# Reordering the loads and the weight splitting at the start of a delta-rule attention and feed-forward kernel

## The chip, the cores and the metric

The kernel runs on one core of one Trainium2 chip. The metric is the device time of one execution in microseconds (us); lower is better. A core has a tensor engine (PE), VectorE (DVE), ScalarE (ACT), GpSimd (POOL) and SyncE (SP), each with an instruction stream of its own that runs strictly in order, and 16 DMA engines that serve the transfers which SP, ACT and POOL issue.

## What is computed

For each of 4 x 8 heads (768 tokens, 48 numbers each) a state matrix is carried along the tokens; the result is reshaped to 3072 tokens of 384 numbers and goes through a feed-forward part:

```python
k_n = k / (norm(k) + 1e-6)
for t in range(S):
    y[t] = q[t] @ state
    state = state + beta[t] * outer(k_n[t], v[t] - state.T @ k_n[t])
x = y, heads side by side                      # (3072, 384)
h = maximum(x @ w_in, 0)                       # w_in (384, 2048)
out = (h * h) @ w_out                          # w_out (2048, 384)
```

The two weight matrices arrive as 64-bit floats, the rest as 32-bit floats.

## The kernel before

**Units.** The tokens are cut into 12 units of 64. Within a unit the recurrence is written as a triangular system: products of keys with keys give a matrix whose 32 x 32 diagonal blocks are inverted, and the inverse (`T`, tile `tt`) is applied to the values. The steps of a unit `d` are: `load` (keys into `kpad`), `load_q`, `load_beta`, `load_v`; `normalize` (squares on ACT at line 268, a chain of small DVE operations, and the scaling of the keys at line 281); `static` (transposes at line 315, copies to `kq` at line 318, products at line 331, copies to `ap` at line 365 for the keys and 375 for the queries, GpSimd selections at line 378); `to_blocks` (line 349), which stores the key products to memory, and `from_blocks` (line 357), which loads their blocks as `lt`; `invert` (lines 417 to 429: a scaling, 31 pairs of DVE operations, a scaling; then the stores at line 433 and the loads at lines 444 and 449 that bring `tt` and `t1t`); `state_part` (`whole`, from the DVE transpose at line 460, `solved`, `onward`); and `moe`, the feed-forward part, from its transposes at line 568 on.

**The two first units.** Units 0 and 1 are inverted together: one `lt` tile holds unit 0's blocks in its lower 64 partitions and unit 1's in its upper 64, and one pass of `invert(ds_[0])` works on both. Their queries sit in `qpad` and in `kpad[2]`, so `load(2)`, which writes the keys of unit 2 to `kpad[2]`, comes after unit 1's queries were transposed.

**Weights.** The weights are 28 pieces in the order in which `moe` needs them: three of `w_in` (128 x 512 numbers, 512 KB) and four of `w_out` (128 x 384, 384 KB), four times over. `fetch(n)` issues the next n transfers on SP. `split_weights` is a generator that turns a piece into a high and a low part: `least` (ACT, line 136) scales the lower words, `words` (four DVE operations, lines 144 to 150) forms the parts, `high` (ACT, line 156), and `low` (tensor engine, lines 163 and 164, and an ACT copy, line 165) forms the low part. While `split_early` holds, one step of the generator takes one piece; afterwards a piece takes three steps, and a further DVE operation (line 170) replaces a matmul.

**Order.** The order of the work is written out by hand at the end of the function (lines 666 to 751), and each engine keeps it. `take(g, n)` runs n steps of a generator. Before, the first 6 weight pieces and unit 0's queries are issued among the key loads, 7 pieces are split before the inverse is written into the order, all 28 pieces are issued before the inverse's stores, 4 pieces are split between the inverse and `whole(ds_[0])`, and 6 within `state_part(ds_[0])` (`EARLY`). The remaining 11 are woven into the stage of unit 1 in `NS` steps, spread over the first 0.88 of the stage beside `moe(ds_[0])`. From then on the stage of unit u weaves `moe` of unit u-1, the state part of unit u, and the inverse of unit u+1.

Of the kernel before, what the change touches and what calls it, by code (L numbers as in the profile page):

```python
# [20 lines left out]
def kernel(  # L21
# [90 lines left out]
    halves = {}  # L112

    rooms = [(spool, "a", "rest"), (mpool, "r", "h_l")]
    AHEAD = 19

    def fetch(n):
        for _ in range(n):
            x = len(raws)
            if x < NW:  # L120
                src = weight_parts[x][2]
                raw = wpool.tile([P, src.shape[1], 2], I32, name=place[x])
                nc.sync.dma_start(out=raw.rearrange("p a b -> p (a b)"), in_=src.bitcast(I32))
                raws.append(raw)
# [5 lines left out]
    def split_weights():  # L130


        def least(x):

            w1 = raws[x][:, :, 1].bitcast(F32)
            nc.scalar.activation(out=w1, in_=w1, func=AF.Copy, scale=DOWN)  # L136
            return x,
# [34 lines left out]
        before, ready, x = None, [], 0  # L172
        while split_early:

            far = 3 if x < AHEAD - 3 else 1
            while len(ready) < far:
                ready.append(least(x + len(ready)))
            if x == 0:
                yield
            now = high(*words(*ready.pop(0)))  # L180
            if before:
                low(*before)
            before = now
            x += 1
            while len(ready) < (far if x < AHEAD - 3 else 1):
                ready.append(least(x + len(ready)))
            yield

# [2 lines left out]
        for x in range(x, NW):  # L191
            if before:
                remainder(*before)
            now = words(*ready.pop(0))
            yield
            if not ready and x + 1 < NW:
                ready.append(least(x + 1))
            yield
            if before:
                low(*before, formed=True)  # L200
            before = high(*now)
            yield
# [35 lines left out]
    def load_q(d):  # L238

        d["qp"] = kpad[2] if d["u"] == 1 else qp  # L240
        load_to(d["qp"], q, d, D)
# [390 lines left out]
    def take(gen, n=None):  # L632
        while n is None or n > 0:
            try:
                next(gen)
            except StopIteration:
                return
            if n is not None:
                n -= 1
# [23 lines left out]
        onward(d)  # L663
        yield

    F0, F1, F2 = 3, 3, 6
    EARLY = (2, 1, 2, 1)
    NS = 3 * (NW + 1 - (1 + 6 + 4 + sum(EARLY))) + 2
    STEPS = 32
    OVER = 4  # L670
    CHAIN = (14.9, 18.4, 21.9, 25.4)
# [6 lines left out]
    engines = {mybir.EngineType.PE, mybir.EngineType.SP, mybir.EngineType.DVE, mybir.EngineType.Activation}  # L678
    with tc.manual_schedule(engines=engines):
        ds_.append(load(0))  # L680
        fetch(F0 - 1)
        ds_.append(load(1))
        fetch(1)
        load_beta(ds_[0])
        load_q(ds_[0])
        load_beta(ds_[1])
        fetch(F1)
        take(normalize(ds_[0]))
        take(normalize(ds_[1]))
        take(splits, 1)  # L690
        pair = [static(d) for d in ds_[:2]]
        for d in pair:
            take(d, 2)
        for d in pair:
            take(d, 1)
        fetch(1)
        for d in pair:
            take(d, 1)
        fetch(2)
        load_q(ds_[1])  # L700
        fetch(F2 - 2)
        load_v(ds_[0])
        take(splits, 1)
        for d in pair:

            take(d, 2)
            take(splits, 1)
            take(d, 1)
            take(splits, 1)
            take(d, 1)  # L710
            take(splits, 1)
        ds_.append(load(2))
        fetch(NW)
        take(invert(ds_[0]))
        load_v(ds_[1])
        load_q(ds_[2])
        load_beta(ds_[2])
        third = normalize(ds_[2])
        take(third, 3)
        for _ in range(3):  # L720
# [61 lines left out]
```

## Time and profile before

| what | us |
|---|---|
| median of three runs | 657.76 |
| lowest and highest run | 652.09, 661.04 |
| profiled execution | 651.91 |
| its span, first to last instruction | 650.1 |

The profiled execution is one run; what it takes outside its span is 1.8 us. Positions in the text are microseconds from the start of this span. PE was busy for 91% of it, VectorE for 66% and ScalarE for 49%.

### The profile page before, as it was taken

How to read it: one execution, taken by the hardware profiler on the slowest of the kernel's cores; microseconds unless marked ns; L12 is line 12 of the kernel's file. 1: busy time of each engine (PE TensorE's matmuls, PEld its weight loads, DVE VectorE, ACT ScalarE, POOL GpSimd, SP SyncE). 2: the span in 40 equal slices, each digit the busy share in tenths (PEclk: the TensorE clock that was granted, in tenths of full speed). 3: DMA queues.
4: the chain of work that ended last, by engine and by line, in shares of the span. 5: the costliest groups of instructions: out<-in, count | busy, mean ns of one | idle time of the engine just before them, and what ended most of it. 6: DMA issues, size and time to landing. Idle time of an engine off the chain costs nothing.

```text
span 650.1 us, 22961 instructions
## 1 busy us (share of the span) xinstructions
PE 588.4 (91%) x9898; PEld 550.0 (85%) x9898; DVE 426.7 (66%) x1154; ACT 315.5 (49%) x620; POOL 37.3 (6%) x61
## 2 busy tenths in 40 slices
PE   0850689889999999999999999999999999999997
PEld 0530268778999999999999999999999999999997
DVE  3889778878479488487496594794884974842221
ACT  3731487555543553645454545435446454444442
POOL 6110000000100100101001001001000010000000
PEclk9956798889999999999999999999999999999999
DMA  7698632401541622722523525317226135030100
GB/s 159 155 247 307 199 63 53 66 3 26 98 70 27 121 58 35 117 52 46 100 52 59 90 45 103 65 28 123 55 41 113 28 51 92 3 63 5 25 2 25
DMA packets 173725, 49.92 MB, mean 77 GB/s; under 512 B 165424, under 2 KB 168504, under 8 KB 173624
## 3 DMA queue, kind: packets, MB, share of 16 engines
q1 hardware_dynamic: 171160, 47.85, 36.8%
q8 instruction: 78, 1.28, 0.8%
q10 hardware_dynamic: 2336, 0.59, 0.5%
q14 instruction: 23, 0.19, 0.1%
q0 software_dynamic: 128, 0.01, 0.0%
HBM read 37.32 MB, written 11.01 MB: 74 GB/s over the span
## 4 chain that ended last, share of the span: by engine, by line
PE 82%; DMA 8%; SPq 3%; DVE 3%; ACT 2%; issue 1%; ACTq 0%; DVEq 0%
PE o L589 32%; PE h L602 31%; DMA w<-in_moe_w_out_dram 2%; PE x L526 2%; PE g L502 2%; PE x L331 2%; PE x L502 2%; PE x L542 2%; DMA kpad<-in_k_dram 2%; PE g L331 2%; PE g L551 1%; SPq L230 1%; DMA inv<-tt 1%; PE x L477 1%; PE h L467 1%
## 5 line engine op out<-in xcount | busy, mean ns | idle before, releaser
L589 PE MATMUL o<-w,h_h 128*128 128x384 f32 x768 | 203.5, 346 | 0.0
L581 DVE TENSOR_TENSOR h_l<-r,h_h 128x512 fp32r<-128x512 f32 x96 | 66.5, 693 | 162.0 <-PE o L589 83.6
L602 PE MATMUL h<-x_h,w 128*128 128x256 f32 x1152 | 171.2, 285 | 0.0
L609 ACT ACTIVATE r<-h 128x512 f32<-128x512 f32 x96 | 57.5, 598 | 219.8 <-PE h L602 219.6
L602 PEld LDWEIGHTS h<-x_h,w 128*128 128x128 f32 x1152 | 156.7, 191 | 1.0
L589 PEld LDWEIGHTS o<-w,h_h 128*128 128x128 f32 x768 | 133.8, 188 | 3.2
L589 PE MATMUL o<-w,h_l 128*128 128x384 f32 x384 | 129.8, 338 | 0.0
L602 PE MATMUL h<-x_l,w 128*128 128x256 f32 x576 | 100.8, 284 | 0.0
L426 DVE SCALAR_TENSOR_TENSOR tmp<-lt,bt,z 128x126 f32<-128x126 f32 (+22 forms) x310 | 95.6, 308 | 7.3
L427 DVE TENSOR_TENSOR z<-z,tmp 128x126 f32<-128x126 f32 (+22 forms) x310 | 79.2, 255 | 10.7
L602 PEld LDWEIGHTS h<-x_l,w 128*128 128x128 f32 x576 | 83.0, 192 | 0.0
L589 PEld LDWEIGHTS o<-w,h_l 128*128 128x128 f32 x384 | 72.2, 188 | 0.0
L610 ACT ACTIVATE r<-r 128x512 f32<-128x512 f32 x96 | 60.7, 632 | 3.0
L612 ACT CAST h_h<-r 128x512 fp32r<-128x512 f32 x96 | 59.5, 620 | 3.1
L410 POOL MEMSET z<- 128x512 f32 x10 | 5.3, 532 | 441.2 <-DMA inv<-z 398.1
L163 PE MATMUL o<-r,plus 128*128 128x512 f32 (+1 forms) x16 | 10.5, 745 | 17.7 <-DVE r L146 17.7
L315 PE MATMUL x<-plus,kpad 64*128 64x64 f32 x104 | 7.5, 245 | 13.9 <-DVE kpad L281 13.9
L331 PE MATMUL x<-kq 48*64 48x64 f32 (+1 forms) x608 | 19.1, 248 | 0.2 <-ACT w L165 0.2
L163 PEld LDWEIGHTS o<-r,plus 128*128 128x128 f32 x16 | 3.0, 233 | 19.2 <-ACT s L271 16.0
L271 ACT ACTIVATE s<-n 128x16 f32<-128x16 f32 x12 | 2.6, 216 | 34.1 <-DVE n L269 34.1
L331 PEld LDWEIGHTS x<-kq 48*64 48x64 f32 x608 | 16.5, 145 | 2.9 <-issue 0.7
L136 ACT ACTIVATE w<-w 128x384 f32<-128x384 f32 (+1 forms) x28 | 17.0, 613 | 2.9 <-DMA w<-in_moe_w_out_dram 2.9
(131 smaller groups left out, 692.9 us busy)
## 6 DMA issues: line engine op xcount, KB each, us to landing
w<-in_moe_w_in_dram SPq DMA_DIRECT2D x12, 512.0 KB
w<-in_moe_w_out_dram SPq DMA_DIRECT2D x16, 384.0 KB
lt<-blocks SPq DMA_DIRECT2D x22, 256.0 KB
vt<-in_v_dram SPq DMA_DIRECT2D x48, 96.0 KB
out_dram<-a SPq DMA_DIRECT2D x46, 96.0 KB
kpad<-in_k_dram SPq DMA_DIRECT2D x88, 48.0 KB
qpad<-in_q_dram SPq DMA_DIRECT2D x88, 48.0 KB
blocks<-ap SPq DMA_DIRECT2D x48, 64.0 KB
```

Source lines behind the costliest of these rows:

```text
L136: nc.scalar.activation(out=w1, in_=w1, func=AF.Copy, scale=DOWN)
L163: nc.tensor.matmul(ps, lhsT=m, rhs=y, start=(m is first[0][0]), stop=False)
L331: nc.tensor.matmul(ps[j][to * C:(to + 1) * C, p, (x - first) * C:(x - first + m) * C], lhsT=kq[rows, c, p, b, 0], rhs=kq[rows, c, p, b, x: ...
L426: nc.vector.scalar_tensor_tensor(out=tmp, scalar=bt[:, s:s + 1], op0=ALU.mult, op1=ALU.mult, **factors)
L427: nc.vector.tensor_tensor(out=z[:, :nj, s + 1:], in0=z[:, :nj, s + 1:], in1=tmp, op=ALU.subtract)
L502: nc.tensor.matmul(dst[j][to, c, p], lhsT=d["kq"][rows, c, p, b, x], rhs=state[rows, b, c, p], start=(c == 0 and p == 0) if x else True, s ...
L581: nc.vector.tensor_tensor(out=h_l, in0=r, in1=h_h.bitcast(F32), op=ALU.subtract)
L589: nc.tensor.matmul(o[i], lhsT=a[:, e, i * P:(i + 1) * P], rhs=halves["wo", ft][w], start=(ft == 0 and n == 0), stop=(ft == FT - 1 and n == 2))
L602: nc.tensor.matmul(hp[:, e], lhsT=halves["wi", (kt, ft // EACH)][w][:, f], rhs=x[:, kt], start=(n == 0), stop=(n == 3 * KT - 1))
L609: nc.scalar.activation(out=r, in_=hp, func=AF.Relu)
L610: nc.scalar.activation(out=r, in_=r, func=AF.Square)
L612: nc.scalar.copy(out=h_h, in_=r)
```

## The change

Both units' keys are issued first; three weight pieces follow. ACT scales no longer three pieces ahead but two. `static` of unit 0 is run as far as `to_blocks` before unit 1's transposes. Four pieces (not seven) are split before the inverse, with one scaled in the first step. Both units' queries, unit 0's values and pieces up to the fifteenth are issued between `from_blocks` and the inverse, and the other 13 pieces behind the loads of `T`, among unit 2's queries, unit 1's values and unit 2's betas. `NS`, the number of weaving steps in the stage of unit 1, goes from 38 to 44, since 14 pieces are left for it where 11 were. `AHEAD` now only says from which piece on both scratch buffers are no longer used in turn.

```diff
-    AHEAD = 19
+    AHEAD = 17
...
         while split_early:
-            far = 3 if x < AHEAD - 3 else 1
-            while len(ready) < far:
-                ready.append(least(x + len(ready)))
             if x == 0:
+                ready.append(least(x))
                 yield
             now = high(*words(*ready.pop(0)))
...
-            while len(ready) < (far if x < AHEAD - 3 else 1):
+            while len(ready) < 2:
                 ready.append(least(x + len(ready)))
             yield
...
-            if not ready and x + 1 < NW:
-                ready.append(least(x + 1))
+            if x + 2 < NW:
+                ready.append(least(x + 2))
...
-    NS = 3 * (NW + 1 - (1 + 6 + 4 + sum(EARLY))) + 2
+    NS = 3 * (NW - (4 + 4 + sum(EARLY))) + 2
...
         ds_.append(load(0))
-        fetch(F0 - 1)
         ds_.append(load(1))
-        fetch(1)
         load_beta(ds_[0])
-        load_q(ds_[0])
+        fetch(3)
         load_beta(ds_[1])
-        fetch(F1)
         take(normalize(ds_[0]))
         take(normalize(ds_[1]))
+        pair = [static(d) for d in ds_[:2]]
+        take(pair[0], 2)
         take(splits, 1)
-        pair = [static(d) for d in ds_[:2]]
-        for d in pair:
-            take(d, 2)
-        for d in pair:
-            take(d, 1)
+        take(pair[0], 1)
+        take(pair[1], 2)
+        take(splits, 1)
         fetch(1)
+        take(pair[1], 1)
+        take(splits, 1)
         for d in pair:
             take(d, 1)
         fetch(2)
+        take(splits, 1)
+        load_q(ds_[0])
+        take(splits, 1)
+        fetch(3)
         load_q(ds_[1])
-        fetch(F2 - 2)
+        fetch(2)
         load_v(ds_[0])
-        take(splits, 1)
+        fetch(4)
         for d in pair:
-            take(d, 2)
-            take(splits, 1)
-            take(d, 1)
-            take(splits, 1)
-            take(d, 1)
-            take(splits, 1)
+            take(d)
         ds_.append(load(2))
+        take(invert(ds_[0]))
+        fetch(2)
+        load_q(ds_[2])
+        fetch(3)
+        load_v(ds_[1])
+        load_beta(ds_[2])
         fetch(NW)
-        take(invert(ds_[0]))
-        load_v(ds_[1])
-        load_q(ds_[2])
-        load_beta(ds_[2])
         third = normalize(ds_[2])
```

## Rows read from the trace of the kernel before

**Rows 1.** The page, parts 1 and 2: busy time of the tensor engine (share of the span, instructions), and its busy tenths in 40 slices of 16.25 us each.

```profile
PE 588.4 (91%) x9898; PEld 550.0 (85%) x9898; DVE 426.7 (66%) x1154; ACT 315.5 (49%) x620; POOL 37.3 (6%) x61
...
PE   0850689889999999999999999999999999999997
```

**Rows 2.** Busy time of each engine in three stretches, cut where the tensor engine begins the transposes of a unit for the feed-forward part (line 568: unit 0 at 93.0 us, unit 1 at 157.0, unit 2 at 202.4). Columns: stretch and its length, then busy us and instructions of PE, PE weight loads, VectorE, ScalarE, GpSimd, then granted clock, DMA share, GB/s.

```profile
0.00:93.00 93.00, 46.17 (x704) 29.21 (x705) 69.87 (x162) 42.01 (x95) 17.16 (x34) 0.80 0.74 196
93.00:157.00 64.00, 53.58 (x831) 48.45 (x830) 51.70 (x126) 38.30 (x77) 0.00 (x0) 0.92 0.24 39
157.00:202.40 45.40, 45.40 (x829) 43.77 (x828) 31.68 (x93) 22.25 (x43) 2.36 (x3) 1.00 0.40 70
```

**Rows 3.** The chain that ended last, in order of time: start, length, what held it.

```profile
1.66 2.98 DMA kpad<-in_k_dram
...
27.62 3.30 DMA blocks<-ap
30.98 0.51 SPq L357
...
63.93 8.22 DMA inv<-tt
```

**Rows 4.** ScalarE's timeline: start, length, line, operation, output and input; in brackets the idle time before and what ended it.

```profile
9.46 0.94 ACT L268 ACTIVATE rest<-kpad 128x384 f32<-128x384 f32 x2 [5.97 <-DMA kpad<-in_k_dram]
...
13.00 0.94 ACT L268 ACTIVATE rest<-kpad 128x384 f32<-128x384 f32 x2 [1.73 <-DMA kpad<-in_k_dram]
...
14.87 1.73 ACT L136 ACTIVATE w<-w 128x512 f32<-128x512 f32 x3
16.50 0.56 ACT L318 COPY kq<-x 128x512 f32<-128x512 f32 x1
...
18.68 0.58 ACT L318 COPY kq<-h 128x512 f32<-128x512 f32 x1 [1.13 <-PE x L315]
...
19.77 0.37 ACT L365 COPY ap<-x 128x256 f32<-128x256 f32 x1
...
22.77 0.38 ACT L365 COPY ap<-x 128x256 f32<-128x256 f32 x1
```

**Rows 5.** VectorE's timeline, in the same columns.

```profile
12.83 0.96 DVE L281 TENSOR_TENSOR kpad<-kpad,s 128x768 f32<-128x768 f32 x1 [0.15 <-DMA kpad<-in_k_dram]
...
16.50 0.96 DVE L281 TENSOR_TENSOR kpad<-kpad,s 128x768 f32<-128x768 f32 x1
17.37 0.42 DVE L144 TENSOR_SCALAR a<-w 128x512 int32<-128x512 int32 x1
...
19.62 0.42 DVE L144 TENSOR_SCALAR r<-w 128x512 int32<-128x512 int32 x1
...
35.84 1.23 DVE L417 TENSOR_TENSOR lt<-lt,bt 128x1024 f32<-128x1024 f32 x1
...
46.09 0.74 DVE L427 TENSOR_TENSOR tt<-tt,h_h 128x247 f32<-128x247 f32 x1
...
47.66 0.42 DVE L427 TENSOR_TENSOR tt<-tt,h_h 128x252 f32<-128x252 f32 x1
...
48.57 0.88 DVE L427 TENSOR_TENSOR tt<-tt,h_h 128x255 f32<-128x255 f32 x1
...
61.97 1.23 DVE L429 TENSOR_TENSOR tt<-tt,bt 128x1024 f32<-128x1024 f32 x1
...
74.74 0.56 DVE L150 SCALAR_TENSOR_TENSOR rest<-w 128x384 fp32r<-128x384 uint32 x1
78.62 0.45 DVE L460 STREAM_TRANSPOSE t<-t1t 128x256 f32<-128x256 f32 x1 [3.32 <-DMA t1t<-inv]
...
108.94 0.35 DVE L144 TENSOR_SCALAR a<-w 128x384 int32<-128x384 int32 x1
...
119.44 0.42 DVE L144 TENSOR_SCALAR a<-w 128x512 int32<-128x512 int32 x1
```

**Rows 6.** SyncE's timeline of transfers issued: start, length over all, line, output and input, count.

```profile
0.81 2.76 SPq L230 DMA_DIRECT2D kpad<-in_k_dram  x4
...
32.63 6.23 SPq L230 DMA_DIRECT2D kpad<-in_q_dram  x8
...
44.02 6.96 SPq L230 DMA_DIRECT2D kpad<-in_k_dram  x8
...
63.93 1.71 SPq L433 DMA_DIRECT2D inv<-tt  x2
72.22 1.93 SPq L444 DMA_DIRECT2D tt<-inv  x4
...
81.15 2.73 SPq L224 DMA_DIRECT2D vt<-in_v_dram  x4
```

**Rows 7.** GpSimd's timeline: the selections that mask the second unit's query products.

```profile
45.66 1.69 POOL L378 TENSOR_SCALAR_AFFINE_SELECT ap<-ap 64x512 f32<-64x512 f32 x2 [13.70 <-ACT ap L375]
48.53 1.44 POOL L378 TENSOR_SCALAR_AFFINE_SELECT ap<-ap 64x512 f32<-64x512 f32 x2 [1.18 <-ACT ap L375]
```

**Rows 8.** Busy time in the stretch 60 to 70 us, columns as in group 2.

```profile
60.00:70.00 10.00, 4.67 (x7) 1.79 (x8) 9.24 (x26) 2.57 (x6) 0.00 (x0) 0.50 1.03 411
```

**Rows 9.** Groups of instructions of the stretch 93 to 157 us by line: busy us, mean ns of one, then the idle time of the engine just before them and what ended it.

```profile
L163 PE MATMUL x<-w,plus 128*128 128x384 f32 (+1 forms) x11 | 5.1, 463 | 8.4 <-DVE w L170 6.1 <-DVE vt L510 2.2
...
L164 PE MATMUL x<-rest,plus 128*128 128x384 f32 (+1 forms) x11 | 4.2, 383 | 0.0
```

More of the change, by code (lines that the diff above doesn't have):

```diff
@@ L664, in state_part @@
         yield
-    F0, F1, F2 = 3, 3, 6
     EARLY = (2, 1, 2, 1)
-    NS = 3 * (NW + 1 - (1 + 6 + 4 + sum(EARLY))) + 2
+    NS = 3 * (NW - (4 + 4 + sum(EARLY))) + 2
     STEPS = 32
```

## The prediction

> **What bounds the kernel now.** I read the page first: the tensor engine is busy for 91% of the span, and its row of slices is at nine tenths from about 150 us to the end; only the first nine slices are thin [rows 1]. The change touches nothing after the stage of unit 1, so the question is when that later part can start. A table by stage says how much there is to win [rows 2]: from 157.0 us a stage lasts 45.4 us and PE is busy for all of it. Before that lie 93.0 us in which PE works 46.17, and a stage of unit 1 of 64.0 us, 18.6 longer than a later one, with VectorE busy for 51.70.
>
> Next the chain that ended last [rows 3] and the timelines of VectorE and SyncE [rows 5, 6]. In the first 93 us the path runs: keys, normalization, key products, their way through memory into `lt`, the inverse on VectorE (35.84 to 63.20, that is 27.36), the inverse's stores, the loads of `tt` and `t1t`, the DVE transpose of line 460 at 78.62, and the state part up to 93.0. Two stalls stand out. From 63.93 the stores of the inverse hold the chain for 8.22; in 60 to 70 us the DMA engines are full (share 1.03, 411 GB/s [rows 8]) with weight pieces issued ahead of those stores. And VectorE stands 3.32 before line 460, for `t1t` [rows 5].
>
> **The change part by part.** I follow four points: start of the inverse, its end, line 460, and the start of unit 0's feed-forward (93.0).
>
> *Start of the inverse (35.84 now).* SP issues a key transfer every 0.69 (2.76 for four [rows 6]), and one lands about 3 after its issue began (2.98 [rows 3]). With nothing but keys in front, two queues of eight are issued by 0.81 + 8 x 0.69 = 6.3, say 6.5 on ACT, whose squares of unit 0 stand behind its issues: 6.6 instead of 9.46 [rows 4]. Squares to scaling of unit 0 take 12.83 - 9.46 = 3.4, and unit 1's scaling follows 3.67 later [rows 5]: 10.0 and 13.7, ended 14.6, if unit 1's keys are there by 10 (they may come up to 2 later, behind the three pieces; before, its squares waited until 13.00 [rows 4]). ACT's first copies of transposed keys (16.50) wait now for three scalings of weights, 14.87 to 16.60 [rows 4]; these go behind them, and the copies come at about 12.6, bound by the transposes: unit 1's scaling ends at 16.50 + 0.96 = 17.46, its copies start at 18.68, 1.2 later [rows 4, 5]. Two copies (1.1), products, and four copies of products (half of 19.77 to 23.15, so 1.7 [rows 4]) put unit 0's stores at about 17. But one inverse serves both units, so what counts is unit 1: two copies, one cast and two scalings (some 0.6 each [rows 4]) and four copies more, about 4.5, so its stores start near 21.5, are issued by 23.7, land 3.3 after the last began (27.62 + 3.30 [rows 3]), at 26.9 or so, and its `lt` load is issued by 27.5. Its landing: from 30.98 to 35.84 is 4.9 at most [rows 3, 5], a key's 2.98 at least. I take 3.5, for only one weight piece stands near it: **31.0**, with ends 29 and 34. VectorE is not late: four pieces (three of 17.37 to 19.62 = 2.25, one narrow of about 1.9 by the ratio of 0.35 to 0.42 of their first operations [rows 5]) from 14.6 with waits for their scalings end near 27. The three pieces it no longer splits here return below.
>
> *Its end (63.20 now).* Length 27.36, but GpSimd stretches it. The operation of line 427 at 46.09 takes 0.74 where a larger one at 47.66 takes 0.42, and at 48.57 one takes 0.88 [rows 5], each beside a GpSimd selection [rows 7]. Now unit 0's four selections run before the inverse and unit 1's four within; after the change all eight queries' selections fall within, since `load_q` of both stands behind `lt`. Four more at about 0.35: +1.4 (bounds 0 and 3.1, the whole of four selections at 0.78). End 31.0 + 27.4 + 1.4 = **59.8**, 3.4 earlier.
>
> The Trainium skill (SBUF — State Buffer, section on the two separate sides) says that the port pair that VectorE and GpSimd share is an exclusive lock, and that the loser blocks for the whole instruction. The rows show operations stretched by 0.3 to 0.5, less than a selection's 0.78. By the rule taken literally the sum would be 1.7 higher than mine.
>
> Is SP free by then? From 27.8 it issues 2 + 3 + 2 + 4 pieces at some 0.5, two sets of queries (6.23), values (2.7) and unit 2's keys (6.96) [rows 6]: 27.6 in all, so 55.4. That is covered by 4.4; each us beyond would delay the stores by one.
>
> *Line 460 (15.4 behind the end now).* Two things must be ready. The transfers: the stores are no longer behind weights. The first load of `tt` starts at 72.22, 8.3 after the stores' issue at 63.93; on idle DMA engines I price that like the stores of blocks, 3.30, and 0.5 for the second store, and 72.22 to 78.62 = 6.4 stays: 0.2 + 3.8 + 6.4 = 10.4. VectorE: it now fills the wait with unit 2's normalization and four pieces until 75.30 [rows 5], 12.1 behind the end. After the change these are pieces 4 to 7, one wide and three narrow instead of three wide and one narrow: 12.1 - 2 x 0.3 = 11.5. So what is late next is VectorE, and line 460 comes at 59.8 + 11.5 = **71.3**: of the 5 us that the transfers save, 3.9 are had.
>
> *Start of unit 0's feed-forward (93.0).* 78.62 to 93.0 is 14.4 with six pieces in it; these have one wide piece fewer: 14.1. **85.4**, so 7.6 earlier.
>
> *The stage of unit 1.* It gets 14 pieces instead of 11. The 18.6 by which it exceeds a later stage, over 11 pieces, is 1.7 each [rows 2]: 3 x 1.7 = **+5.1**. From below: PE's own share, (5.1 + 4.2)/11 = 0.85 each [rows 9], 2.5. From above: between 108.94 and 119.44 VectorE begins a piece every 3.5 [rows 5], 10.5 for three. I take the middle, since VectorE is busy for 81% of the stage: neither free nor full. PE waits for the pieces here (8.4 ahead of line 163, 6.1 of it for VectorE [rows 9]).
>
> *The 13 late pieces.* Cost nothing, if covered: `T`'s loads occupy SP for 81.15 - 72.22 = 8.9 [rows 6], so from about 63.7 to 72.6; with queries, values, betas and pieces SP has issued the last at about 92, and eight pieces of 3.5 MB need 8.6 at 411 GB/s [rows 8]. Piece 20, first of these, lands near 94 and is scaled a quarter into the stage, near 102. If SP slips by more than 8, ACT waits there, and all its copies with it.
>
> Sum: -7.6 + 5.1 = **-2.5** on the profiled execution's 651.91, that is 649.4. That execution was near the fastest of the runs; against their median of 657.76 the same step gives **655.3**.
>
> **The rivals.** *Pieces nearly free.* VectorE has 12.3 idle in the stage [rows 2]; if the moved pieces fall there, only PE's 2.5 remains: -5.1, 652.7 (with an inverse at 29, -7.1). For: in this stage VectorE's idle time is in waits that more pieces can fill. Against: its first part has none.
>
> *VectorE bounds the stage of unit 1* (the other side). Place: the weave of pieces, inverse and remainders behind 85 us. If the stage is VectorE's, each piece costs its spacing, 3.5, and 10.5 - 7.6 = +2.9: 660.7. It decides once a piece costs over 2.5. For: 81% busy, PE waiting for it. Against: later in the stage it waits for PE.
>
> *The first blocks' early departure does nothing.* Both halves of `lt` are scaled at once, and unit 1's way is now behind unit 0's products. If its `lt` lands at 35.8 as before, the inverse ends at 64.6 and line 460 at 76.1, 2.5 earlier; with 0.3 and +5.1: +2.3, 660.1. For: the shared tile. Against: the keys and ACT's scalings ahead of it move by 3 to 4.
>
> **How the numbers follow.** Forecast 0.47, pieces nearly free 0.27, VectorE's stage 0.18, blocks late 0.08. By these the step lies between -8 and +3, 649.8 to 660.8; the three runs shown spread from 5.7 below to 3.3 above their median, so some of that goes on both ends: 646 to 662. The forecast's own range is -5 to 0. Two per cent, about what a measurement of this kernel can tell from no change, is 13 us: faster by that would need the whole gain, a free stage and a lucky set of runs, 0.07; slower by that needs the full price of the pieces and late weights, 0.04; the rest, 0.89, lies within.
>
> **What would show it.** Right: line 417 at 29 to 33; the inverse some 28.8 long with eight selections beside it; stores to first `tt` load in under 4.5; line 460 at 70 to 73 with no wait for `t1t` ahead of it; line 568 first at 84 to 87; then 67 to 71 us to unit 1's line 568. Wrong: line 417 still near 35; SP reaching the stores late; or ACT waiting for weight pieces of `w_out` behind 95 us. A stage of unit 1 of 66 us or less means the first rival, of 74 the second.

## The result: 0.56% slower, and where the time went

| what | before | after |
|---|---|---|
| median of 20 runs, us | 653.89 | 657.44 |
| lowest and highest run, us | 650.76, 661.04 | 654.70, 661.73 |
| profiled execution, us | 651.91 | 661.73 |
| start of unit 1's feed-forward in it (line 568 before, 566 after), us | 157.0 | 161.0 |

The ratio is 1.0056 with a 95% interval of 1.0036 to 1.0076: a small loss, where a small gain was forecast. The 657.76 us from which the prediction started was the median of three runs; twenty give 653.89. So 655.3 lies near 657.44 by luck, because the base was high, and the step, -2.5 for a measured +3.55, has the wrong sign.

In the code after, all lines from 230 on have numbers lower by two: 417 is 415, 460 is 458, 568 is 566. The page first, as in [rows 1]: PE is busy for 593.5 us where it was 588.4, and its thin slices now reach to the tenth.

```profile
PE 593.5 (90%) x9892; PEld 555.4 (84%) x9892; DVE 430.8 (65%) x1157; ACT 316.4 (48%) x620; POOL 36.1 (5%) x61
...
PE   2553878778999999999999999999999999999997
```

The stretches of after, cut at the same points as [rows 2] (line 566: unit 0 at 84.4 us, unit 1 at 161.0, unit 2 at 206.5), and one later stage. Columns as there.

```profile
0.00:84.40 84.40, 43.35 (x694) 27.71 (x694) 64.27 (x150) 38.19 (x86) 16.88 (x34) 0.78 0.70 170
84.40:161.00 76.60, 59.04 (x839) 53.45 (x838) 60.82 (x143) 42.96 (x86) 0.00 (x0) 0.87 0.37 83
161.00:206.50 45.50, 45.50 (x831) 43.88 (x830) 31.14 (x90) 22.32 (x43) 2.30 (x3) 1.00 0.41 69
298.80:347.60 48.80, 47.32 (x829) 45.43 (x828) 31.96 (x93) 22.25 (x43) 1.96 (x3) 0.97 0.37 65
```

The first stretch is 8.6 shorter, the second **12.6 longer**: 4.0 lost at 161.0, which the medians confirm with 3.55. The other 5.8 by which the two profiled executions differ are in later stages, where both kernels do the same. After's profiled execution is the slowest of its 20, with a stage of 48.8 in it, and the medians do not bear this part out; the last section returns to it.

The steps of the first stretch, in VectorE's timeline (start, length, line, operation, idle time before), to be held against [rows 5]:

```profile
30.29 1.23 DVE L415 TENSOR_TENSOR lt<-lt,bt 128x1024 f32<-128x1024 f32 x1 [3.37 <-DMA lt<-blocks]
...
38.78 0.77 DVE L425 TENSOR_TENSOR tt<-tt,h_h 128x231 f32<-128x231 f32 x1
...
41.91 0.42 DVE L425 TENSOR_TENSOR tt<-tt,h_h 128x247 f32<-128x247 f32 x1
...
57.65 1.23 DVE L427 TENSOR_TENSOR tt<-tt,bt 128x1024 f32<-128x1024 f32 x1
...
69.11 0.69 DVE L150 SCALAR_TENSOR_TENSOR h_l<-w 128x512 fp32r<-128x512 uint32 x1
69.72 0.44 DVE L458 STREAM_TRANSPOSE t<-t1t 128x256 f32<-128x256 f32 x1
```

SyncE's stores of the inverse and the first loads of `tt`, against [rows 6]; GpSimd's selections, against [rows 7]; ScalarE's first squares, first copy of transposed keys and first scaling of a weight behind it, against [rows 4]:

```profile
58.96 1.13 SPq L431 DMA_DIRECT2D inv<-tt  x2
62.01 1.93 SPq L442 DMA_DIRECT2D tt<-inv  x4
```

```profile
38.65 2.96 POOL L376 TENSOR_SCALAR_AFFINE_SELECT ap<-ap 64x512 f32<-64x512 f32 x4 [27.24 <-ACT ap L373]
46.17 3.12 POOL L376 TENSOR_SCALAR_AFFINE_SELECT ap<-ap 64x512 f32<-64x512 f32 x4 [4.56 <-ACT ap L373]
```

```profile
6.63 0.94 ACT L266 ACTIVATE rest<-kpad 128x384 f32<-128x384 f32 x2 [3.14 <-DMA kpad<-in_k_dram]
...
13.48 0.59 ACT L316 COPY kq<-x 128x512 f32<-128x512 f32 x1
...
14.44 0.68 ACT L136 ACTIVATE w<-w 128x512 f32<-128x512 f32 x1
```

The inverse starts at 30.29 (35.84 before) and ends at 57.65 + 1.23 = 58.88 (63.20). From its stores to the loads behind them it is 62.01 - 58.96 = 3.05, where it was 8.29. Line 458 comes at 69.72, right behind VectorE's last operation on a piece (69.11), with no wait for `t1t`.

Then the stage of unit 1. Groups by line of PE for 84.4 to 161.0, as in [rows 9], and the longest waits there (engine and line, what it waited for: us in total, times, longest):

```profile
L163 PE MATMUL x<-w,plus 128*128 128x384 f32 (+1 forms) x14 | 6.7, 476 | 15.7 <-DVE w L170 12.8 <-DVE vt L508 2.9
L164 PE MATMUL x<-rest,plus 128*128 128x384 f32 (+1 forms) x13 | 5.1, 396 | 0.0
```

```profile
ACT w L165 <- PE x L164: 17.3, 8, 4.3
PE x L163 <- DVE w L170: 12.8, 8, 2.7
...
DVE w L170 <- ACT w L156: 4.1, 7, 1.0
```

PE's idle time ahead of line 163 went from 8.4 [rows 9] to 15.7, which is all by which its idle time in the stage grew (64.00 - 53.58 = 10.4 to 76.60 - 59.04 = 17.6). PE's busy time grew by 5.5: three pieces at 0.87 (6.7/14 + 5.1/13) are 2.6, and the other 2.9 come with a mean granted clock of 0.87 where it was 0.92 [rows 2]. So **12.6 = 7.1 of waiting + 2.6 of own work + about 2.9 of slower work.** The list of waits shows a ring: PE waits for VectorE's line 170, that for ScalarE, and ScalarE for PE.

Waiting and slow work belong together. First PE's timeline, its matmuls of line 163 from 133 to 155 us; then four stretches around one of them (columns as in [rows 2]):

```profile
133.61 0.47 PE L163 MATMUL x<-w,plus 128*128 128x512 f32 x1 [2.41 <-DVE w L170]
...
139.01 0.35 PE L163 MATMUL x<-w,plus 128*128 128x384 f32 x1
...
144.13 0.44 PE L163 MATMUL x<-w,plus 128*128 128x384 f32 x1 [2.50 <-DVE w L170]
...
150.41 0.33 PE L163 MATMUL x<-w,plus 128*128 128x384 f32 x1
...
154.71 0.41 PE L163 MATMUL x<-w,plus 128*128 128x384 f32 x1 [2.73 <-DVE w L170]
```

```profile
139.00:141.60 2.60, 2.60 (x18) 2.43 (x17) 1.99 (x5) 0.89 (x2) 0.00 (x0) 1.00 0.00 0
141.60:144.10 2.50, 0.03 (x1) 0.00 (x0) 2.40 (x7) 0.00 (x0) 0.00 (x0) 1.00 0.01 3
145.40:148.40 3.00, 3.00 (x94) 2.78 (x94) 2.83 (x9) 2.26 (x4) 0.00 (x0) 0.50 0.00 0
149.00:152.00 3.00, 2.98 (x38) 2.60 (x30) 2.71 (x7) 1.75 (x4) 0.00 (x0) 1.00 0.32 56
```

One piece is ready when PE comes to it, and for the next PE stands 2.4 to 2.7. Before and during such a wait the granted clock is 1.00 (2.4 GHz); about a microsecond after PE starts again it is 0.50 (1.2 GHz), for over 3 us in which PE is busy throughout, and then 1.00 again. Three us at half speed do the work of 1.5, so this wait costs 2.5 and then some 1.5 more. The stage has five waits of over 2 us (2.56, 2.88, 2.41, 2.50 and 2.73), each with such a stretch in or right behind it, and no slow stretch elsewhere.

### The profile page after: what moved, and what is told of

Read it like the earlier page. It is cut to its first block, busy times and chain, and to the rows that moved or that the text cites. A ratio compares the mean times of both kernels' runs of the same rounds, so it can differ in the third digit from the quotient of the medians.

```text
span 659.7 us, 22948 instructions
## 1 busy us (share of the span) xinstructions
PE 593.5 (90%) x9892; PEld 555.4 (84%) x9892; DVE 430.8 (65%) x1157; ACT 316.4 (48%) x620; POOL 36.1 (5%) x61
## 4 chain that ended last, share of the span: by engine, by line
PE 82%; DVE 8%; DMA 4%; ACT 2%; issue 2%; SPq 1%; DVEq 0%; ACTq 0%
PE o L587 32%; PE h L600 31%; PE g L500 2%; DVE tt L425 2%; DVE h_h L422 2%; PE x L540 2%; PE x L329 2%; PE x L524 2%; PE g L549 2%; PE x L500 2%; PE g L329 2%; PE x L475 1%; PE h L465 1%; PE h L566 1%; PE x L313 1%
## 5 line engine op out<-in xcount | busy, mean ns | idle before, releaser
L329 PE MATMUL x<-kq 48*64 48x64 f32 (+1 forms) x608 | 21.3, 264 | 1.3 <-ACT kq L316 1.3
L329 PEld LDWEIGHTS x<-kq 48*64 48x64 f32 x608 | 18.7, 159 | 3.5 <-ACT kq L316 2.1
L163 PE MATMUL x<-w,plus 128*128 128x384 f32 (+1 forms) x14 | 6.7, 476 | 15.7 <-DVE w L170 12.8
L163 PE MATMUL o<-a,plus 128*128 128x384 f32 (+1 forms) x14 | 9.0, 736 | 12.4 <-DVE a L146 12.2
L163 PEld LDWEIGHTS x<-w,plus 128*128 128x128 f32 x14 | 2.8, 201 | 18.2 <-issue 10.9
```

The lines of the kernel that those rows point to most:

```text
L163: nc.tensor.matmul(ps, lhsT=m, rhs=y, start=(m is first[0][0]), stop=False)
L329: nc.tensor.matmul(ps[j][to * C:(to + 1) * C, p, (x - first) * C:(x - first + m) * C], lhsT=kq[rows, c, p, b, 0], rhs=kq[rows, c, p, b, x: ...
```

## The experiments

**Theory:** the price of a piece in the stage of unit 1 is no average. The first four runs were made with a price of some 4 us a piece at any count in mind; from `b_early9` on the theory was that up to some eleven pieces fill gaps and each one beyond costs some 4 us, whatever came before the stage. **Rivals:** the late pieces arrive late or disturb the stage as transfers; the front of the program (order of loads, earlier inverse) changed something else; VectorE's load, its density or the clock sets the price. In what follows "a/b/c" are pieces split in the state part, pieces left for the stage, and weaving steps; before is 6/11/38, after 6/14/44.

**1. The count.** `early9`: after, with three pieces moved back into the state part (9/11/38). The 38 steps are those of before; the change's own formula would give 35 for eleven pieces, which experiment 5 tries.

```diff
-    EARLY = (2, 1, 2, 1)
-    NS = 3 * (NW - (4 + 4 + sum(EARLY))) + 2
+    EARLY = (3, 2, 2, 2)
+    NS = 38
```

> The changed kernel with three more pieces split within the state part of unit 0 (nine, not six), so that 11 pieces are left for the stage of unit 1, in the 38 weaving steps of the kernel before. Theory: the stage of unit 1 pays some 4.2 us for each of the three added pieces (76.6 after the change, 64.0 before, over 3), while a piece in the state part costs VectorE's 2.1. Then unit 0's feed-forward starts near 91 (84.4 + 6.4), the stage is back at 64 to 65, unit 1's starts near 155, and the time is 6 us below the changed kernel, some 2 below the one before. Rival, late weights and a fuller queue: 13 pieces still come behind T, so the stage stays at 73 to 77 and the time is some 6 above the changed kernel.

`late17`: after, with three more left for the stage (3/17/53).

```diff
-    AHEAD = 17
+    AHEAD = 12
...
-    EARLY = (2, 1, 2, 1)
+    EARLY = (1, 0, 1, 1)
```

> The changed kernel with three pieces fewer in the state part of unit 0 (three, not six), so 17 in the stage of unit 1, in 53 steps; the scratch buffers change over at piece 12. Theory of a price per piece: unit 0's feed-forward starts 6.4 earlier, near 78, and the stage grows by another 12.6 to about 89, so 6 us above the changed kernel. Rival, late weights: the stage already waits for the weights' landing and not for the splitting, so three more pieces cost it 3 or less beyond, and the time is 2 to 4 below the changed kernel.

The stretches from line 458 to unit 0's line 566, and from there to unit 1's, first of `early9`, then of `late17`:

```profile
69.30:89.80 20.50, 16.13 (x291) 9.05 (x290) 18.45 (x39) 16.47 (x36) 0.00 (x0) 1.00 0.65 157
89.80:154.30 64.50, 51.37 (x831) 45.39 (x830) 51.56 (x126) 38.72 (x78) 0.00 (x0) 0.97 0.39 94
```

```profile
69.50:83.70 14.20, 11.09 (x267) 7.55 (x266) 6.86 (x15) 8.04 (x18) 0.00 (x0) 0.76 0.67 190
83.70:174.00 90.30, 66.42 (x845) 58.81 (x844) 67.01 (x158) 47.76 (x95) 0.00 (x0) 0.81 0.32 73
```

Stage lengths 64.5, 76.6 and 90.3 for 11, 14 and 17 pieces: 4.0 and 4.6 a piece, the 4.0 with the change of steps in it. (Which scratch buffers the first late pieces use also differs, by `AHEAD`: before and after have one piece in the second pair in this stage, `early9` has none. Before's 64.0 and `early9`'s 64.5 show no effect of that.) The 12.1 between `early9` and after are 4.4 of PE's waiting (13.1 to 17.6), 2.6 of own work and 5.1 of slower work, with a granted clock of 0.97 for 0.87. In the state part three pieces cost 14.7 - 14.2 = 0.5 (from 3 to 6) and 20.5 - 14.7 = 5.8 (from 6 to 9). `early9` took 650.31 us, 0.9949 of before (0.9913 to 0.9986): **the change with eleven pieces in 38 steps is faster than both kernels, by about half a percent and one percent.** `late17` took 673.71, 1.0288 (1.0223 to 1.0353).

**2. The count without the rest of the change.** `b_split4`: before, with three pieces fewer split ahead of the inverse, so that the stage gets 14 (6/14/44); all weights arrive early and the front is before's.

```diff
-    AHEAD = 19
+    AHEAD = 17
...
-    NS = 3 * (NW + 1 - (1 + 6 + 4 + sum(EARLY))) + 2
+    NS = 3 * (NW - (4 + 4 + sum(EARLY))) + 2
...
+            n = 1 if d is pair[0] else 0
             take(d, 2)
-            take(splits, 1)
+            take(splits, n)
...
-            take(splits, 1)
+            take(splits, n)
...
-            take(splits, 1)
+            take(splits, n)
```

> The kernel before with three pieces fewer ahead of the inverse (four, not seven), 14 in the stage of unit 1, in 44 steps as after the change; all loads as before, so every weight has landed by 72. Theory of a price per piece: the inverse starts at 35.5 all the same, since unit 1's blocks land then, the stage is 76 to 77, and the time is 10 to 12 us above the kernel before. Rival, late weights: no weight is late here, so the stage stays at 64 to 69 (PE's 0.85 to 1.7 a piece), 0 to 5 above the kernel before.

Its stage, 92.66 to 168.2:

```profile
92.66:168.20 75.54, 58.53 (x837) 53.05 (x836) 60.78 (x143) 42.39 (x85) 0.00 (x0) 0.86 0.20 33
```

75.5 us, 11.5 over before's 64.0, at 668.41 us (1.0213, 1.0152 to 1.0274). No weight is late here, and with late weights `early9` has 64.5: the rival of late transfers falls. The long stage goes with 14 pieces in 44 steps.

`b_early9`: before, with `EARLY = (3, 2, 2, 2)` and `AHEAD = 22` (9/8/29).

```diff
-    AHEAD = 19
+    AHEAD = 22
...
-    EARLY = (2, 1, 2, 1)
+    EARLY = (3, 2, 2, 2)
```

> The kernel before with nine instead of six pieces split in the state part of unit 0, so 8 instead of 11 in the stage of unit 1. The runs so far have a stage of 64 to 65 us at 11 pieces, 76 at 14 and 90 at 17. Theory of a marginal price that rises with the load: below 11 the stage still has slack, a piece costs the average that the forecast used, 1.7, the stage shrinks by about 5 to 59, the state part grows by 5.5, and the time is that of the kernel before, within 1.5. Rival, a constant price of 4.2: the stage shrinks to 51.5 and the time is 7 us below the kernel before.

`early12`: after, with 12/8/29.

```diff
-    AHEAD = 17
+    AHEAD = 23
...
-    EARLY = (2, 1, 2, 1)
-    NS = 3 * (NW - (4 + 4 + sum(EARLY))) + 2
+    EARLY = (4, 3, 3, 2)
+    NS = 29
```

> The changed kernel with twelve pieces split in the state part of unit 0, 8 left for the stage of unit 1. Theory of a price that rises with the load: 8 pieces make a stage of 59 to 60 (as in the kernel before with 8 left), the state part grows by 5.5 over that with nine (90 to 95.5), and the time equals that of the version with nine, within 1.5, unless ScalarE waits for pieces 18 to 21, which land at 84 to 95; then 1 to 4 above it. Rival, constant price of 4.2: the stage falls to 52 and the time is 7 us below the version with nine.

With eight pieces the stage lasts 59.6 and 59.4 us, so from eight to eleven a piece costs 1.5 to 1.7 (29 and 38 steps, both by before's formula). In the state part the same three cost 5.4 (before) and 6.5 (after). Times: `b_early9` 652.24, 0.9955 (0.9932 to 0.9977); `early12` 651.14, 0.9955 (0.9930 to 0.9980). Both beat before, but neither beats `early9` clearly: below eleven, a piece is worth about the same in the state part.

**3. The stores' queue alone.** `b_rest_behind`: before, where only the later weights go behind the loads of `T` (6/11/38).

```diff
-        fetch(NW)
+        fetch(2)
         take(invert(ds_[0]))
-        load_v(ds_[1])
+        fetch(2)
         load_q(ds_[2])
+        fetch(3)
+        load_v(ds_[1])
         load_beta(ds_[2])
+        fetch(NW)
```

> The kernel before with only the queue changed: 15 pieces are issued ahead of the inverse's stores, 13 behind the loads of T in the order of the changed kernel; 7, 4 and 6 pieces are split at the old places, 11 in the stage. Theory of a price per piece: the stores no longer stand behind weights, line 460 comes 3 earlier (VectorE's four pieces end then), the stage keeps its 64 to 65, and the time is 3 us below the kernel before. Rival, late weights: the stage grows by 6 to 12 though its pieces are 11, and the time is 3 to 9 above.

Line 460 came at 74.23, 4.4 earlier, but unit 0's line 568 at 92.84, as before: the state part took 18.6 for 14.4. Time 654.15, 0.9986 (0.9954 to 1.0019). Before's code scales pieces three ahead, and the piece it wants in the state part is now behind `T`. ScalarE's timeline shows the wait for it; behind it the stretch 82 to 88 us, columns as in [rows 2].

```profile
80.68 0.68 ACT L136 ACTIVATE w<-w 128x512 f32<-128x512 f32 x1 [1.28 <-DMA w<-in_moe_w_in_dram]
```

```profile
82.00:88.00 6.00, 5.93 (x69) 4.45 (x69) 2.84 (x5) 4.67 (x12) 0.00 (x0) 0.51 0.79 201
```

ScalarE's wait is 1.3. For PE the 4.2 are 1.6 of idle time (3.2 for 1.6) and 2.6 of busy time (15.4 for 12.8): it was busy throughout these 6 us at a granted clock of 0.51, where in before, from 84 to 90 us, the clock was 1.00. So with before's order of scaling, moving the weights gained nothing.

**4. What sets the price above eleven.** Each run takes one suspect away from after. (In experiment 5 a shift of the steps by 0.03 alone moves this stage by 6 us, so a difference of 2 in one of these runs names no cause by itself.)

`pool_rem`: the remainder of line 170 on GpSimd, off VectorE.

```diff
-            nc.vector.tensor_tensor(out=hl[:, 1], ...
+            nc.gpsimd.tensor_tensor(out=hl[:, 1], ...
```

> The changed kernel with the remainder of the 14 late pieces (0.56 to 0.69 us each on VectorE) done by GpSimd, which is idle in this stage. Theory, VectorE's load sets the stage: 14 x 0.6 = 8 us come off it, and the stage falls from 76.6 by 5 to 8. Rival, the stage is bound by the relay of each piece from engine to engine (ScalarE, VectorE, TensorE in turn, each in order): GpSimd's operation takes as long or longer, the stage stays at 75 to 80.

```profile
L170 POOL TENSOR_TENSOR w<-a,w x13: 993/1215/1802, 91.4 to 152.7; 128x384 fp32r<-128x384 f32 x8, 128x512 fp32r<-128x512 f32 x5
```

Above, the group of line 170 in the list for that line (count, then shortest, mean and longest ns). It takes 1.2 us on GpSimd, where VectorE took 0.55 to 0.69; VectorE's own busy time in the stage did not fall (62.4 us for 60.8, with 15 instructions fewer), so it was not relieved. The stage is 74.7, 1.9 less, the time 656.06 (1.0012, 0.9979 to 1.0044).

`no146`: the operation of line 146 left out for the late pieces.

```diff
-            nc.vector.scalar_tensor_tensor(out=a, in0=w1, ...
+            if split_early:
+                nc.vector.scalar_tensor_tensor(out=a, in0=w1, ...
```

> The changed kernel without the second operation of the splitting (the signs of the weights) in the 14 late pieces, which leaves the signs of these weights out; it takes 14 x 0.6 = 8.5 us from VectorE and 0.6 from each piece's way. Theory, from 11 pieces on VectorE's work and the relay through it set the stage: it falls from 76.6 by 6 to 9, to 68 to 70. Rival, TensorE sets it, by its own work at half clock: it falls by 3 or less.

```profile
83.50:158.30 74.80, 58.04 (x839) 52.17 (x838) 52.34 (x129) 42.73 (x86) 0.00 (x0) 0.86 0.38 88
```

VectorE works 52.34 in the stage for 60.82, yet the stage (above) is 74.8: 8.5 us of work taken away, 1.8 won. 656.76 us, 1.0038 (1.0004 to 1.0071). **Less work for VectorE does not by itself shorten the stage.**

`low_later`: PE's matmuls of lines 163 and 164 one weaving step later, so that PE meets them when VectorE is further on.

```diff
-        before = None
+        before = prior = None
...
+            if prior:
+                low(*prior, formed=True)
+            prior = before
...
-            if before:
-                low(*before, formed=True)
...
+        low(*prior, formed=True)
```

> The changed kernel with the two matmuls that form a late piece's low part one weaving step later in the order, behind the next piece's turn, so TensorE reaches them some 1.5 us later. Theory, the relay: TensorE's wait at line 163 (some 24 us in the stage for VectorE) shrinks by a half or more and the stage falls by 5 or more. Rival, VectorE's load sets the stage: TensorE only waits elsewhere, and the stage keeps 74 to 78.

Stage 75.1, time 657.88 (1.0025, 0.9992 to 1.0057): -1.5 in the stage, and the time shows nothing.

`spread97`: the 44 steps over 0.97 of the stage.

```diff
-                parts.append((splits, steps(NS, 0, 0.88)))
+                parts.append((splits, steps(NS, 0, 0.97)))
```

> The changed kernel with the 14 pieces woven over 0.97 of the stage instead of 0.88. Theory of a price per piece, whatever the density: the stage stays within 2 of 76.6. Rival, the density (44 steps in the room of 38) makes the price: it falls by 4 or more.

Stage 77.6, time 660.14 (1.0069, 1.0031 to 1.0106). Standing less densely did not shorten it.

`warm4`: four extra matmuls ahead of each late low part, whose result is overwritten.

```diff
+            if formed:
+                for _ in range(4):
+                    nc.tensor.matmul(ps, lhsT=plus, rhs=halves["wi", (0, 0)][0][:, :hl.shape[2]], start=True, stop=True)
```

> The changed kernel with four further matmuls ahead of each late piece's low part, whose result is overwritten; they add 14 x 4 x 0.2 = 11 us of TensorE work where it often waits. Theory, VectorE's work and the relay set the stage: the matmuls fill waits, the granted clock rises from 0.87, and the stage stays within 3 of 76.6. Rival, the lower clock makes the price (TensorE's work at half speed): the stage falls by 3 or more. Third way, TensorE is the bound: it grows by 6 to 11.

```profile
84.10:159.80 75.70, 62.33 (x893) 56.11 (x892) 60.52 (x143) 43.15 (x86) 0.00 (x0) 0.98 0.36 84
```

The granted clock rose from 0.87 to 0.98 and PE's idle time fell from 17.6 to 75.70 - 62.33 = 13.4, but its busy time rose from 59.0 to 62.3 in spite of the clock: the extra matmuls took what the rest gave, and the stage is 75.7. As a cure this is void. As evidence it says that waits need not bring slow stretches: of waits of 2.0 to 2.8 us four are left in the stage, but only one slow stretch, of 3.5 us. 665.69 us, 1.0181 (1.0140 to 1.0221), more than the stage explains: later stages were long too (47.4 and 49.0).

`inv_out`: unit 2's inverse moved whole out of the stage, into the next one.

```diff
-                parts.append((inverse, steps(NI - n_i, 0, I1 - 1) + [0.16]))
+                parts.append((inverse, steps(NI if u == 2 else NI - n_i, 0, 0.3 if u == 2 else I1 - 1) + [0.32 if u == 2 else 0.16]))
...
-            if inverse:
+            if inverse and u > 1:
```

> The changed kernel with unit 2's inverse taken out of the stage of unit 1 (all of it in the first 0.3 of the next stage, which grows). If remainders that wait on VectorE behind the inverse make the price: the stage of unit 1 falls from 76.6 by 5 or more. If it is the pieces against the feed-forward alone: by 3 or less.

The stage and the next one:

```profile
83.70:152.20 68.50, 55.60 (x839) 49.53 (x838) 48.85 (x99) 42.69 (x86) 0.00 (x0) 0.90 0.41 93
152.20:230.70 78.50, 51.21 (x831) 48.79 (x830) 43.65 (x134) 22.37 (x43) 1.96 (x3) 0.80 0.23 40
```

8.1 us less in the stage, the largest gain of any run with 14 pieces; the next stage pays 33 for it (681.92, 1.0399, 1.0274 to 1.0524). Twelve us of VectorE's work gone gave 8.1, where 8.5 gone in `no146` gave 1.8. Why, VectorE's timeline shows at the wait of 2.50 above: first after, then the same place in `no146` (where 579 is line 580 and 170 is 171) and in `inv_out`.

```profile
140.68 0.69 DVE L579 TENSOR_TENSOR h_l<-r,h_h 128x512 fp32r<-128x512 f32 x1 [0.48 <-PE o L587]
...
143.52 0.55 DVE L170 TENSOR_TENSOR w<-a,w 128x384 fp32r<-128x384 f32 x1
```

```profile
138.35 0.69 DVE L580 TENSOR_TENSOR h_l<-r,h_h 128x512 fp32r<-128x512 f32 x1 [1.66 <-ACT w L157]
...
141.19 0.55 DVE L171 TENSOR_TENSOR w<-a,w 128x384 fp32r<-128x384 f32 x1
```

```profile
137.39 0.69 DVE L579 TENSOR_TENSOR h_l<-r,h_h 128x512 fp32r<-128x512 f32 x1 [0.77 <-PE o L587]
...
138.87 0.55 DVE L170 TENSOR_TENSOR w<-a,w 128x384 fp32r<-128x384 f32 x1
```

Between the two stand, in after and in `no146`, four operations of unit 2's inverse and the scaling of its keys: 2.84 from one start to the other in both. What `no146` saved ahead of them VectorE spends waiting (1.66). In `inv_out` the four are gone and it is 1.48. PE's last three waits in the stage for line 170 are 2.41, 2.50 and 2.73 in after, 2.41, 2.49 and 2.73 in `no146`, 0.81, 1.12 and 1.41 in `inv_out`, which has no slow stretch there either. So at these places it matters which operations VectorE has ahead of a piece's line 170, not how much work it has in all.

**5. Placement.** Six runs change how the pieces stand against the rest of the weave. `early9_low_later` is `early9` with the edit of `low_later`:

> Nine pieces in the state part of unit 0, 11 in the stage, and their low parts formed one weaving step later. By the run of the later step with 14 pieces (stage 75.1, not 76.6): 1 to 1.5 us off the stage of 64.5, so 649 us. If at 11 pieces TensorE bounds the stage more than VectorE, no difference: 650 to 651.

`early8` has one piece fewer in the state part than `early9` (8/12/38):

```diff
-    AHEAD = 17
+    AHEAD = 19
...
-    EARLY = (2, 1, 2, 1)
+    EARLY = (3, 2, 2, 1)
```

> The changed kernel with eight pieces in the state part of unit 0, 12 in the stage of unit 1. Gradual price: the stage lasts 68 to 69. Placement: it may lie anywhere from 64 to 72, off the line between 64.5 (11) and 76.6 (14) by 2 or more.

`early9_35` and `early9_44` are `early9` with 35 steps, the number that the change's formula gives for eleven pieces, and with 44:

```diff
-    NS = 38
+    NS = 3 * (NW - (4 + 4 + sum(EARLY))) + 2
...
-    NS = 38
+    NS = 44
```

> Nine pieces in the state part, 11 in the stage, in 35 weaving steps instead of 38, so that the same 11 end at 0.88 of the stage and not at 0.81. If only the number counts: a stage of 64 to 65, 650 us. If the places count: it differs from 64.5 by 2 or more, either way.

> Nine pieces in the state part, 11 in the stage, in 44 steps, so that they end at 0.70 of the stage. If an earlier end goes on helping: a stage of 60 to 63 and 646 to 649 us. If 0.81 was early enough and only the density grows: 64 to 67 and 650 to 653.

`phase03` is after with the steps shifted, `ns47` after with 47 steps:

```diff
-                parts.append((splits, steps(NS, 0, 0.88)))
+                parts.append((splits, steps(NS, 0.03, 0.91)))
```

> The changed kernel, 14 pieces in the stage, all weaving steps 0.03 of the stage later. If only the number counts: 76 to 77.5. If the places count: it differs from 76.6 by 2 or more, either way.

```diff
-    NS = 3 * (NW - (4 + 4 + sum(EARLY))) + 2
+    NS = 47
```

> The changed kernel with 47 weaving steps instead of 44 (the old formula's 3 x 14 + 5), so that its 14 pieces end at 0.82 of the stage and not at 0.88. If the three lost steps make half of the price: the stage falls from 76.6 to 69 to 71, the time by 6, to 651 to 652. If the number of pieces makes it: 75 to 77.

The stages of these runs, and of those above that change only counts, steps or loads (PE idle and the mean granted clock are of the stage):

| run | pieces, steps | stage, us | PE idle, us | clock | median, us | ratio (95%) |
|---|---|---|---|---|---|---|
| early12 | 8, 29 | 59.4 | 9.2 | 0.91 | 651.14 | 0.9955 (0.9930-0.9980) |
| b_early9 | 8, 29 | 59.6 | 9.1 | 0.91 | 652.24 | 0.9955 (0.9932-0.9977) |
| before | 11, 38 | 64.0 | 10.4 | 0.92 | 653.89 | 1 |
| early9 | 11, 38 | 64.5 | 13.1 | 0.97 | 650.31 | 0.9949 (0.9913-0.9986) |
| b_rest_behind | 11, 38 | 65.1 | 12.7 | 0.95 | 654.15 | 0.9986 (0.9954-1.0019) |
| early9_44 | 11, 44 | 66.2 | 12.8 | 0.90 | 650.98 | 0.9971 (0.9944-0.9998) |
| early9_low_later | 11, 38 | 69.9 | 15.0 | 0.88 | 656.44 | 1.0046 (1.0024-1.0067) |
| early9_35 | 11, 35 | 71.1 | 16.7 | 0.90 | 656.62 | 1.0048 (1.0020-1.0076) |
| early8 | 12, 38 | 73.1 | 14.6 | 0.86 | 654.83 | 1.0001 (0.9974-1.0028) |
| low_later | 14, 44 | 75.1 | 17.8 | 0.91 | 657.88 | 1.0025 (0.9992-1.0057) |
| b_split4 | 14, 44 | 75.5 | 17.0 | 0.86 | 668.41 | 1.0213 (1.0152-1.0274) |
| after | 14, 44 | 76.6 | 17.6 | 0.87 | 657.44 | 1.0056 (1.0036-1.0076) |
| spread97 | 14, 44 | 77.6 | 18.4 | 0.85 | 660.14 | 1.0069 (1.0031-1.0106) |
| ns47 | 14, 47 | 80.2 | 20.1 | 0.85 | 661.12 | 1.0108 (1.0057-1.0158) |
| phase03 | 14, 44 shifted | 82.6 | 18.6 | 0.81 | 660.70 | 1.0098 (1.0069-1.0128) |
| late17 | 17, 53 | 90.3 | 23.9 | 0.81 | 673.71 | 1.0288 (1.0223-1.0353) |

So the theory was half right. More pieces cost more, but **the same eleven take 64.0 to 71.1 us, and the same fourteen 75.1 to 82.6, by where they and their matmuls stand in the order alone**, and the long ones have more waiting, a lower clock, or both.

This bears on experiment 1. Before's formula gives n pieces 3n + 5 steps, the change's 3n + 2. By the change's, 11, 12, 14 and 17 pieces (`early9_35`, `early8`, after, `late17`) take 71.1, 73.1, 76.6 and 90.3: 1.8 a piece up to 14, 4.6 beyond. By before's, 8, 11 and 14 (`early12`, `early9`, `ns47`) take 59.4, 64.5 and 80.2: 1.7, then 5.2. (Width does not order these prices: the three pieces between 8 and 11 and those between 14 and 17 are narrow, the three between are wide.) So the 4.0 of experiment 1 is the price by neither, and how much of the 12.6 is due to the count depends on the steps at which one compares; yet the new formula is not the culprit either, since after with the old one (`ns47`) got longer. And three pieces moved back at the change's own formula (`early9_35`) gained nothing clear of noise (1.0048, after 1.0056): the gain of `early9` needs the 38 steps too.

What a bad place looks like stands in `early9_35`: its stage, then VectorE around 120 us, then PE there and at its longest wait.

```profile
89.80:160.90 71.10, 54.38 (x833) 48.97 (x832) 52.13 (x128) 38.72 (x78) 0.00 (x0) 0.90 0.36 85
```

```profile
120.08 0.69 DVE L579 TENSOR_TENSOR h_l<-r,h_h 128x512 fp32r<-128x512 f32 x1 [2.17 <-PE o L587]
...
121.16 0.68 DVE L170 TENSOR_TENSOR w<-a,w 128x512 fp32r<-128x512 f32 x1
...
124.37 0.98 DVE L508 TENSOR_TENSOR vt<-vt,x 128x384 f32<-128x384 f32 x2
```

```profile
120.53 0.52 PE L600 MATMUL h<-x_l,w 128*128 128x256 f32 x3
125.03 0.77 PE L163 MATMUL x<-w,plus 128*128 128x512 f32 x1 [3.99 <-DVE vt L508]
...
153.81 0.66 PE L163 MATMUL x<-w,plus 128*128 128x384 f32 x1 [4.86 <-DVE w L170]
```

VectorE stands 2.17 before line 579, for PE's line 587; only then can it run line 170 of one piece (121.16), behind that the four operations of the next and a transpose, and then line 508 (124.37). PE's line 163 needs a buffer of `x`, which line 508 still reads; so PE, done at 121, stands 3.99 for it. Each engine waits for the other in turn, because each keeps its written order. In `early9` the same wait for line 508 is 2.2 us, in `ns47` 5.1 and in `phase03` 4.9. It is not the only such place: `early8` has 2.2 here, but like `early9_35` one wait of 4.86 for line 170 late in the stage, where `early9` has none over 1.9 us behind 125.

What is shown: beyond 2.6 us of PE's own work the loss consists of PE's stops at line 163, most of them for VectorE's line 170, and of stretches at half clock behind them; it grows with the count, by an amount that the places decide; it doesn't follow VectorE's load as a whole. What stays open: from which count on, and at which places, the stops arise. Nothing here would forecast them.

## Why the prediction was wrong

- **Start of the inverse**, predicted 31.0: 30.29. The squares came at 6.63 (6.6 forecast), the first copy of keys at 13.48 (12.6), with the weights' scalings behind it, as forecast.
- **Its end**, 59.8: 58.88. All eight selections fell within, length 28.59, so four more cost 1.2 where 1.4 was taken: the operation beside one takes 0.77, another 0.42. The Trainium skill (SBUF — State Buffer, section on the two separate sides) has the shared port pair locked for a whole instruction; taken literally, by my estimate, that would have given up to 3.1, and the trace does not agree with it.
- **Line 460 (458)**, 71.3: 69.72. The stores landed sooner than estimated (3.05 for 3.8), and VectorE was late next, as said: 10.8 behind the inverse's end, 11.5 forecast.
- **Unit 0's feed-forward**, 85.4: 84.4. The step is -8.6 for -7.6.
- **The late pieces** were covered: ScalarE never waited for a weight in the stage. In `b_rest_behind`, which scales three ahead, it waited 1.3 for one, in the state part.
- **The stage of unit 1 is the step that failed**: +5.1 forecast, +12.6 measured. I divided the 18.6 by which the stage exceeded a later one by its 11 pieces and took this average of 1.7 as the price of three more. Only PE's own share was right (2.5 for 2.6). The average held from 8 to 11 pieces (1.5 to 1.7 each) and not from before to after: there 7.1 of new waiting and 2.9 of slower work came on top, 4.2 a piece in all. My own bound from above, 10.5, was too low: it was VectorE's spacing in a stretch in which PE waited only 0.97 for it. Nor had I a term for the clock, nor one for the places: the same fourteen pieces take 75.1 to 82.6, and at eleven pieces three steps fewer cost 6.6 (64.5 to 71.1), where I had put the new number of steps at nothing without a reason. With 12.6 in place of 5.1 the sum is +5.0 on my terms, +4.0 with the measured gain.

Of the rivals, the second came about by its own mark (a stage of 74 or more, a piece over 2.5), but not by its reason: VectorE is busy for 60.82 of 76.60, 79% for 81% before, and `no146` took 8.5 us of work off it for 1.8. The first and third are false: pieces were not nearly free, and the blocks did arrive early.

## What to carry to other kernels

The price of one more item in a stage woven from several in-order engines is not the stage's excess over its items: count what it costs to add and to remove three, before work is moved there, and at more than one placement, since here 8 to 11 cost 1.6 each, and 11 to 14 cost 1.8 or 5.2 each by the steps in which they were woven. When time won at the start is paid for by moving work into a later stage, try the other places too (here three pieces cost 5.8 in the state part, and that paid only together with the right steps). And before a load is taken off the engine that others wait for, look at what stands ahead of the awaited operation in that engine's order: 8.5 us of VectorE's work gone gave 1.8.

## What the runs showed of the hardware

- In after's profiled execution the stage from 298.8 to 347.6 us lasts 48.8, where unit 2's lasted 45.5. PE stands idle in the middle of a run of matmuls and its wait has no releaser; the stage's granted clock is 0.97, 1.00 elsewhere. PE's timeline there:

```profile
328.10 0.60 PE L500 MATMUL g<-state,kq 48*64 48x48 f32 x25 [1.48 <-issue]
```

  Later stages of 47 to 49 us stand in `warm4` too. Before's profile has none; what causes it is open.
- In after, PE waited 2.4 to 2.9 us five times and each time ran some 3 us and more at 1.2 GHz behind it, though busy (141.6 to 148.4 above). It is no rule: in `before` such a stretch follows a wait of 1.8 (at 134.7), in `pool_rem` none follows one of 3.1 (at 153.7). In `early9` waits of up to 2.2 stand in the stage too, and its clock is 0.97; the sum of waiting does not decide, for before has less of it (10.4 for 13.1) and a lower clock (0.92). What decides is open.
- An operation moved from VectorE to GpSimd gave VectorE nothing back: with 14 remainders on GpSimd (17.7 us busy there) VectorE's other operations took longer, 62.4 us in all for 60.8.
